# Linear attention with a channel-mix layer on one core: new instruction orders, wk columns read with a step, and two batches mixed on TensorE

## Chip, core and metric

The kernel runs on one core of a Trainium2 chip. The metric is the device time of one execution in microseconds. The engines are called by the names of the profile: PE is TensorE, DVE VectorE, ACT ScalarE, POOL GpSimd and SP SyncE. PEld is PE's weight load, which can run beside a matmul.

## What is computed

```python
# q, k, v: (8 batches, 8 heads, 576 rows, 64)
q_s = softmax(q, over the 64)
k_s = softmax(k, over the 576 rows)
kv  = einsum('bhsd,bhse->bhde', k_s, v)
x   = einsum('bhsd,bhde->bhse', q_s, kv)        # heads side by side: (8, 576, 512)
x_prev = x shifted by one row (zeros ahead of row 0)
xk = mu_k * x + (1 - mu_k) * x_prev
xr = mu_r * x + (1 - mu_r) * x_prev
k  = maximum(xk @ w_k, 0)                       # w_k: 512 x 1024
v  = (k * k) @ w_v                              # w_v: 1024 x 512
out = sigmoid(xr @ w_r) * v                     # w_r: 512 x 512
```

All inputs and the output are float32; the kernel multiplies in bf16.

## The kernel before

**Attention.** For each batch b and each of two groups g of four heads, `attention(b, g)` (L403) adds these steps. ACT takes the exponentials of q and k (L413) and casts v to bf16 (L419); DVE sums the exponentials of q by row, takes reciprocals and scales (L426, L429, L434); PE transposes the scaled q (L465, 36 small matmuls, each with its own weight load) into a PSUM bank `att`, and ACT copies it to `qt` (L470). PE multiplies k and v (L443, 36 small matmuls, the kv step) into another `att` bank (for batch 0 into two `mm` banks), and DVE takes the reciprocal of k's sums (L450, L454). These small matmuls use the PE array as four parts of 64x64.

**Mixing rows.** For the batches named in `ON_PE` (L36, only batch 0), DVE makes weights that hold kv, the reciprocal and mu or 1 - mu (`wps`, L515), and PE adds the present and the shifted rows in one bank: two pieces (h = 0, 1) for each of xk and xr (m = 0, 1), of 12 and 8 matmuls (L478 through L521). Each piece is evicted to `xk` or `xr` by the engine that `EVAC` names (L529). For the other batches PE makes x in two plain pieces of 4 matmuls (`w`, L556), ACT copies them to `xb` (L564), and DVE does the edge, the difference, four scalings by mu and two sums (L569 to L583).

**Channel mix.** Half of the batches (2304 rows) lie in a ring; `unit` (L613) takes them in pieces of 512, 512, 512, 512 and 256 rows. Per unit there are eight k steps (one for each 128 of the 1024 columns of w_k: four matmuls with a slice of `wk_bf` as weights and 512 or 256 rows of `xk` moving, L640), each followed by relu on ACT (L625) and a square on DVE (L629). Then, for each 128 rows, an r step (four matmuls, L671), tanh on ACT (L676), two v steps of four matmuls (L681), the gating on DVE (L687) and two stores from SP (L697). In the first two units of the first half, a k step is two halves: channel blocks 0 and 2, which need group 0, and 1 and 3, which need group 1. Four PSUM banks `mm` serve k, r and v; two pairs of banks `att` serve the attention.

**Loads.** The first batch's q, k and v come through ACT's and SP's queues in the order of `FIRST` (L30). All else is issued by POOL: wk in two parts (cast to bf16 on the way, each waiting for the load that `GATE` numbers), wr, the small mu load, wv in two parts, and the further batches, into 12 `raw` buffers.

**What sets the order.** No order is written out by hand. Each step is an `Op` with an engine, an occupation and a latency in microseconds, a key (due time) and the buffers that it takes. `Plan.order` (L120) walks a clock: for each engine it ranks what can start by start time (those within `LOOK` of the engine's free time count as equal) and key, and takes the earliest. `set_due` (L101) passes due times back from a step to what it needs, with `SPARE` more at each; `AHEAD` makes the mixes of batch 0, 1 and later due so much earlier; `PACE` spaces the due times of the matmuls. While PE was not busy for over 2.0 us of the last 3.4, its steps count twice. The order found is emitted as a fixed program.

Of the kernel before, what the change touches and what calls it, by code (L numbers as in the profile page):

```python
# [16 lines left out]
START = 0.7  # L17
HOP = 0.05
LATE = 1e6
SPARE = 0  # L20
LOOK = {"PE": 0.03, "ACT": 0.2, "DVE": 0.1, "POOL": 0.03, "SP": 0.03}
AHEAD = (1.0, 4, 8)
MAIN = 17.0
PACE = 1.148
DMA_RATE = 365.0
DMA_LEAD = 2.5
DMA_TAIL = 0.6

PARTS = {1: [slice(0, 2)], 2: [slice(0, 1), slice(1, 2)]}
FIRST = ((0, 0, ("ACT", "ACT")), (1, 0, ("SP", "SP")), (0, 1, ("ACT", "SP")),  # L30
         (0, 2, ("SP", "SP")), (1, 1, ("SP", "SP")), (1, 2, ("SP", "SP")))
ORDER = (0, 1, 2)
SOON = {(1, 0, 0): 2.2, (1, 0, 1): 2.4, (1, 1, 0): 2.7, (1, 0, 2): 3.5}
GATE = 6
FILL = 0
ON_PE = (0,)  # L36
CASTS = (("ACT", "ACT"), ("ACT", "ACT"))
EVAC = ((("ACT", "DVE"), ("ACT", "ACT")), (("ACT", "DVE"), ("ACT", "ACT")))


class Slot:
# [8 lines left out]
class Op:  # L50


    def __init__(self, engine, occ, lat, key, emit, deps, takes, gives, size):
        self.engine, self.occ, self.lat, self.key = engine, occ, lat, key
        self.emit, self.deps, self.takes, self.size = emit, list(deps), list(takes), size
        self.start = self.end = None
        self.early = 0.0
        for slot in gives:
            slot.last.append(self)


class Plan:
# [57 lines left out]
    def order(self):  # L120
        self.set_due()
        free = {}
        self.pe_busy = []
        dma_free = 0.0
        waiting = {}
        for op in self.ops:
            waiting.setdefault(op.engine, []).append(op)
        done = []
        left = len(self.ops)
        while left:  # L130
            chosen = None
            for engine, ops in waiting.items():
                now = free.get(engine, START)
                ready = None
                for op in ops:
                    if any(d.end is None for d in op.deps):
                        continue
                    t = max([now] + [d.end + HOP for d in op.deps])
                    ok = True
                    for slot in op.takes:  # L140
                        got = self.slot_time(slot)
                        if got is None:
                            ok = False
                            break
                        t = max(t, got[0] + HOP)
                    if not ok:
                        continue
                    rank = (max(t, now + LOOK[engine]), op.key)
                    if ready is None or rank < ready[0]:
                        ready = (rank, t, op)  # L150
                if ready is not None and (chosen is None or ready[1] < chosen[1]):
                    chosen = ready
            assert chosen is not None, "no operation can start"
            _, t, op = chosen
            for slot in op.takes:
                slot.index = self.slot_time(slot)[1]
                for part in self.pools[slot.pool][slot.index]:
                    self.user[part] = slot
            occ, lat = op.occ, op.lat
            if op.engine == "PE" and not self.warm(t):  # L160
                occ, lat = 2 * occ, occ + lat
            op.start, op.end = t, t + lat
            if op.size and op.size < 20:
                op.end = t + lat + (2.0 if op.engine == "SP" else 8.0)
            elif op.size:
                dma_free = max(dma_free, t + DMA_LEAD) + op.size / DMA_RATE
                op.end = dma_free + DMA_TAIL
            if op.engine == "PE":
                self.pe_busy.append((t, t + occ))
            free[op.engine] = t + occ  # L170
            waiting[op.engine].remove(op)
            done.append(op)
            left -= 1
        return sorted(done, key=lambda o: o.start)
# [3 lines left out]
def kernel(  # L178
# [81 lines left out]

    queues = {"SP": nc.sync, "ACT": nc.scalar, "POOL": nc.gpsimd}
    loaded = {}

# [22 lines left out]
    def emit_mu_load():  # L288
        for m, src in enumerate((moe_mu_k, moe_mu_r)):
            ap = bass.AP(tensor=src.tensor, offset=src.offset, ap=[[128, 4], [1, 128]])  # L290
            nc.gpsimd.dma_start(out=mu_sb[4 * m:4 * m + 4, :], in_=ap)

    def emit_warm():
        nc.scalar.activation(out=warm[:], in_=warm[:], func=ACT.Exp)
# [15 lines left out]
            nc.vector.memset(t[:, :, 0:1], 0.0)  # L310

    zero = plan.add("DVE", 0.1, 0.15, -10, emit_warm_zero)
    plan.add("ACT", 1.6, 1.7, 3.5, emit_warm, [zero])
    identity = plan.add("POOL", 0.6, 0.8, -9.1, emit_identity)
    consts = plan.add("DVE", 0.2, 0.3, -9, emit_consts, [identity])
    late_consts = plan.add("DVE", 0.14, 0.2, LATE, emit_late_consts)
# [16 lines left out]
                         rhs=mu_rows[:].rearrange("p m c -> p (m c)"), start=True, stop=True)  # L333

    def emit_mu_wide():
        nc.scalar.copy(out=mu_all[:, :, 0, :, :].rearrange("p m g c -> p m (g c)"),
                       in_=bank(rows_slot).rearrange("p (m c) -> p m c", m=2))

    def emit_mu_rest(m):
        nc.gpsimd.tensor_scalar(out=mu_all[:, m, 1, :, :], in0=mu_all[:, m, 0, :, :],  # L340
# [1 line left out]

    rows_load = plan.add("SP", 0.9, 0.9, -600, emit_mu_rows_load, size=10.0)
    rows_done = plan.add("PE", 0.86, 0.98, -501, emit_mu_rows, [rows_load, consts], [rows_slot])
    wide = plan.add("ACT", 0.48, 0.6, 0, emit_mu_wide, [rows_done], [], [rows_slot])
    mu_split = [plan.add("POOL", 0.5, 0.6, -2 + m, lambda m=m: emit_mu_rest(m), [wide])
                for m in range(2)]

# [24 lines left out]

    wk_done, wv_done = [], []
    for g in range(2):
        wk_done.append(plan.add("POOL", 0.75, 0.75, g, lambda g=g: emit_wk(g), gate,
                                size=1048.0))
    wr_done = plan.add("POOL", 0.75, 0.75, 2, emit_wr, gate, size=1048.0)
    mu_load = plan.add("POOL", 1.2, 1.2, 2.05, emit_mu_load, gate, size=8.0)
    mu_t = plan.add("PE", 0.2, 0.4, LATE, emit_mu, [mu_load, consts], [mu_slot])  # L380
    mu_done = plan.add("DVE", 0.08, 0.17, LATE, emit_mu_copy, [mu_t], gives=[mu_slot])

    def emit_wv(h):
        n = FT // 2
        ap = bass.AP(tensor=moe_w_v.tensor, offset=moe_w_v.offset + h * n * 128 * C,
                     ap=[[C, 128], [128 * C, n], [1, C]])
        nc.gpsimd.dma_start(out=wv_bf[:, h * n:(h + 1) * n, :], in_=ap)

    for h in range(2):
        wv_done.append(plan.add("POOL", 0.75, 0.75, 3 + h, lambda h=h: emit_wv(h), gate,  # L390
                                size=1048.0))
    for b in range(1, B):
        for g in range(2):
            for n, i in enumerate(ORDER):
# [8 lines left out]
    def attention(b, g):  # L403
# [63 lines left out]
                            in_=qss[qs.index][r, j, 64 * u:64 * u + 64], identity=ident[r, r])  # L467

        def copy_qt():
            nc.scalar.copy(out=qts[qt.index][:], in_=transposed()[:, :, 0:S])  # L470

        def by_heads(xp, parts):

# [13 lines left out]
        for n, u in enumerate(us):  # L487
# [10 lines left out]
            expk.append(plan.add("ACT", 0.09 + 0.96 * f, 0.2 + 0.96 * f, step + 1,  # L498
                                 lambda u=u: exp(eks, ek, sk, u), [lk[n]], [ek] if one else [],
                                 [sk]))  # L500
            if CASTS[min(b, 1)][n] == "ACT":
                castv.append(plan.add("ACT", 0.09 + 0.95 * f, 0.2 + 0.96 * f, step + 2,
                                      lambda u=u: cast_v(nc.scalar.copy, u), [lv[n], consts],
                                      [vv] if one else [], [sv]))
            else:
                castv.append(plan.add("DVE", 0.07 + 1.2 * f, 0.15 + 1.2 * f, step + 2,
                                      lambda u=u: cast_v(nc.vector.tensor_copy, u),
                                      [lv[n], consts], [vv] if one else [], [sv]))
        tr = plan.add("PE", 0.45, 0.62, pe_key, transpose_q, scaled + [identity], [qtp], [qs])
        qcopy = plan.add("ACT", 1.0, 1.12, step + 3, copy_qt, [tr], [qt], [qtp])  # L510
        kvm = plan.add("PE", 0.5, 0.6, pe_key, kv, expk + castv, [kvp], [ek, vv])
        zdone = plan.add("DVE", 0.08 * (2 if b == 0 else 1), 0.25 if b == 0 else 0.16, step + 2, recz, [kvm], [rz])

        def weights_of(wp, m, hf):
# [10 lines left out]
                     ((now, 0, 0, HS), (then, 0, 64, HS), (then, S - 64, 1, 64)))  # L525

        def copy_mixed(engine, xp, m, h):
            copy = nc.scalar.copy if engine == "ACT" else nc.vector.tensor_copy
            copy(out=xs[m][:, g::2, c0 + HS * h:c0 + HS * h + HS], in_=bank(xp)[:, :, 0:HS])  # L529

        if on_pe:
            for m in range(2):
# [6 lines left out]
                        for hf in range(2)]  # L539
                for h in range(2):  # L540
                    xp = Slot("att")
                    o = plan.add("PE", 0.29, 0.46, pe_key,
                                 lambda wp=wp, xp=xp, h=h: x_mixed(wp, xp, h), [qcopy] + made,
                                 [xp], [qt, wp])
                    e = EVAC[min(b, 1)][m][h]
# [36 lines left out]
        def mix(m):  # L582
# [1 line left out]
                                    in0=xms[xms_[m].index][:], in1=xbs[xb.index][:, :, 0:S],  # L584
                                    op=ALU.add)

        wdone = plan.add("DVE", 0.25, 0.35, step + 4, weights, [zdone, late_consts], [w],
                         [kvp, rz])
        evs = []
        for h in range(2):  # L590
            o = plan.add("PE", 0.16, 0.35, pe_key, lambda h=h: x(h),
                         [qcopy, wdone], [xps[h]], [qt, w])
            evs.append(plan.add("ACT", 0.52, 0.64, step + 5, lambda h=h: copy_x(h), [o],
                                [xb] if h == 0 else [], [xps[h]]))
# [18 lines left out]
    def unit(half, c0, n):  # L613
# [24 lines left out]
        def k_part(kf, fc, cts):  # L638
            for ct in cts:
                nc.tensor.matmul(bank(kf)[:, 0:n],  # L640
                                 lhsT=wk_bf[:, ct, fc * 128:(fc + 1) * 128],
                                 rhs=xs[0][:, ct, c0:c0 + n],
                                 start=(ct == 0), stop=(ct == CT - 1))

# [119 lines left out]
```

## Time and profile before

| | |
|---|---|
| median of 6 runs | 211.42 us (210.85 to 213.04) |
| the profiled execution: its time / its span | 211.94 / 210.2 us |
| PE busy | 187.3 us (89%) |
| PE weight loads busy | 90.1 us |
| DVE busy | 152.3 us (72%) |
| ACT busy | 150.6 us (72%) |
| POOL busy | 39.5 us |
| read from memory / written to it | 33.56 / 9.44 MB |
| share of PE in the chain that ended last | 76% |

The span runs from the first to the last recorded instruction; the execution's own time has 1.74 us more around it. In a timeline row stand the start, the duration, the engine, the line, the operation, what it writes and reads, the shape and how many rows were merged; in square brackets how long the engine stood idle before it and what, by the semaphores, ended that. A matmul's duration includes its way through the array, so the pace of matmuls is read from the distance of their starts. The granted clock is the share of full speed that PE was given. DMA moves nearly all the time until about 105 us, at about 400 GB/s between 35 and 75 us.

### The profile page before, as it was taken

The page shows a single profiled execution, that of the slowest core. Times are in us where ns is not written, and L with a number is a line of the kernel's source. Part 1 is how long each engine was busy: PE and PEld are TensorE (multiplying, and loading weights), DVE is VectorE, ACT ScalarE, POOL GpSimd, SP SyncE. Part 2 cuts the span into 40 slices and gives each one's busy share as a digit, 9 for nine tenths or more (in the row PEclk, how much of TensorE's full clock was granted, in tenths as well). Part 3 has the DMA queues.
Part 4 walks back from the last instruction along what each step waited for, and adds up shares of the span by engine and source line. Part 5 has one row for each costly group of instructions (what it writes and reads, how often), then busy time and mean ns, then how long its engine had stood idle before and what let it go on. Part 6 is the DMA issues. An engine that isn't in the chain of part 4 may idle for free.

```text
span 210.2 us, 5164 instructions
## 1 busy us (share of the span) xinstructions
PE 187.3 (89%) x2073; PEld 90.1 (43%) x2099; DVE 152.3 (72%) x338; ACT 150.6 (72%) x229; POOL 39.5 (19%) x63
## 2 busy tenths in 40 slices
PE   3188998948999989999997999999999999999991
PEld 0064444413444444454446443445444444444740
DVE  2683593999989999997749974976797369632531
ACT  4793998988999799999566987337993872452440
POOL 1471836534425112431000000000000000000000
PEclk9999999996999999999999999999999999999998
DMA  6999999999999997899442031242034103402514
GB/s 211 353 261 233 301 219 366 387 409 402 390 395 408 403 390 289 291 393 339 132 106 47 5 78 22 50 101 53 3 76 101 27 21 76 106 3 51 122 28 100
DMA packets 15856, 40.72 MB, mean 194 GB/s; under 512 B 2252, under 2 KB 3800, under 8 KB 15832
## 3 DMA queue, kind: packets, MB, share of 16 engines
q0 software_dynamic: 8336, 27.40, 38.9%
q1 hardware_dynamic: 7064, 12.10, 21.0%
q10 hardware_dynamic: 432, 0.88, 1.4%
q8 instruction: 16, 0.26, 0.5%
q14 instruction: 8, 0.07, 0.1%
HBM read 33.56 MB, written 9.44 MB: 205 GB/s over the span
## 4 chain that ended last, share of the span: by engine, by line
PE 76%; ACT 9%; DVE 9%; DMA 3%; issue 2%; ACTq 0%; DVEq 0%
PE mm_b L640 8%; PE mm_d L640 8%; PE mm_b L681 7%; PE mm_d L681 7%; PE mm_a L681 7%; PE mm_c L681 7%; PE mm_c L640 6%; PE mm_a L640 5%; PE mm_a L671 5%; PE mm_c L671 4%; PE mm_b L671 3%; DMA raw_b<-in_k_dram 3%; PE att_a L478 2%; PE att_b L478 2%; DVE qs_a L434 2%
## 5 line engine op out<-in xcount | busy, mean ns | idle before, releaser
L640 PEld LDWEIGHTS <-wk_bf 128*128 128x128 bf16 x320 | 30.8, 100 | 33.6 <-issue 5.7
L640 PE MATMUL mm_b<-xk,wk_bf 128*128 128x512 bf16 (+1 forms) x91 | 23.4, 365 | 1.8 <-DVE xk L583 1.7
L640 PE MATMUL mm_d<-xk,wk_bf 128*128 128x512 bf16 (+1 forms) x94 | 24.0, 368 | 0.2
L681 PEld LDWEIGHTS <-k_b 128*128 128x128 bf16 x144 | 13.5, 98 | 16.6 <-issue 1.1
L671 PEld LDWEIGHTS <-xr 128*128 128x128 bf16 x144 | 13.7, 98 | 15.8
L681 PEld LDWEIGHTS <-k_a 128*128 128x128 bf16 x144 | 13.3, 98 | 15.7 <-issue 0.9
L640 PE MATMUL mm_c<-xk,wk_bf 128*128 128x512 bf16 (+1 forms) x66 | 16.9, 365 | 0.6 <-issue 0.6
L640 PE MATMUL mm_a<-xk,wk_bf 128*128 128x512 bf16 (+1 forms) x60 | 14.9, 366 | 0.0
L671 PE MATMUL mm_a<-wr_bf,xr 128*128 128x512 bf16 x51 | 13.3, 379 | 0.1
L676 ACT ACTIVATE th_a<-mm_a 128x512 f32<-128x512 f32 x12 | 7.3, 607 | 6.5 <-PE mm_a L671 6.5
L671 PE MATMUL mm_c<-wr_bf,xr 128*128 128x512 bf16 x43 | 11.3, 380 | 0.1
L681 PE MATMUL mm_d<-wv_bf,k_a 128*128 128x512 bf16 x37 | 10.0, 379 | 0.6 <-issue 0.2
L681 PE MATMUL mm_b<-wv_bf,k_b 128*128 128x512 bf16 x37 | 10.0, 380 | 0.3 <-DVE rz_c L450 0.2
L681 PE MATMUL mm_a<-wv_bf,k_a 128*128 128x512 bf16 x39 | 10.1, 380 | 0.2 <-issue 0.2
L629 DVE TENSOR_TENSOR k_a<-rel_a 128x512 bf16<-128x512 bf16 (+1 forms) x13 | 5.1, 391 | 6.9 <-ACT rel_a L625 6.8
L681 PE MATMUL mm_d<-wv_bf,k_b 128*128 128x512 bf16 x39 | 9.9, 379 | 0.0
L676 ACT ACTIVATE th_b<-mm_c 128x512 f32<-128x512 f32 x8 | 4.9, 608 | 6.4 <-PE mm_c L671 6.3
L625 ACT ACTIVATE rel_b<-mm_d 128x512 bf16<-128x512 f32 (+1 forms) x12 | 7.1, 592 | 2.8 <-PE mm_d L640 2.2
L681 PE MATMUL mm_c<-wv_bf,k_b 128*128 128x512 bf16 x31 | 8.2, 380 | 0.1
L681 PE MATMUL mm_b<-wv_bf,k_a 128*128 128x512 bf16 x32 | 8.2, 379 | 0.0
L681 PE MATMUL mm_a<-wv_bf,k_b 128*128 128x512 bf16 x32 | 8.2, 379 | 0.0
L681 PE MATMUL mm_c<-wv_bf,k_a 128*128 128x512 bf16 x29 | 7.9, 380 | 0.3 <-DVE qs_b L434 0.2
(251 smaller groups left out, 420.1 us busy)
## 6 DMA issues: line engine op xcount, KB each, us to landing
out_dram<-ot_a SPq DMA_DIRECT2D x24, 128.0 KB, 2.4
out_dram<-ot_b SPq DMA_DIRECT2D x24, 128.0 KB, 2.4
out_dram<-ot_c SPq DMA_DIRECT2D x24, 128.0 KB, 2.4
raw_a<-in_q_dram POOLq DMA_DIRECT2D x3, 576.0 KB, 11.3
raw_c<-in_k_dram POOLq DMA_DIRECT2D x2, 576.0 KB, 10.4
raw_b<-in_v_dram POOLq DMA_DIRECT2D x2, 576.0 KB, 10.9
raw_d<-in_q_dram POOLq DMA_DIRECT2D x2, 576.0 KB, 10.8
raw_e<-in_k_dram POOLq DMA_DIRECT2D x2, 576.0 KB, 11.5
```

The source lines that it names most:

```text
L434: nc.vector.tensor_tensor(out=to[:, :, u, :], in0=eqs[eq.index][:, :, u, :], in1=by[:, :, :, None].to_broadcast((128, J, u.stop - u.start, ...
L478: nc.tensor.matmul(bank(xp)[64 * hf:64 * hf + 64, u, c:e], lhsT=w[r, hf, :], rhs=qts[qt.index][r, hf, src:src + e - c], start=(n == 0), st ...
L625: nc.scalar.activation(out=rels[rel.index][:, 0:n], in_=bank(kf)[:, 0:n], func=ACT.Relu, scale=HALF_ROOT)
L629: nc.vector.tensor_tensor(out=k2s[k2.index][:, fc, 0:n], in0=rels[rel.index][:, 0:n], in1=rels[rel.index][:, 0:n], op=ALU.mult)
L640: nc.tensor.matmul(bank(kf)[:, 0:n], lhsT=wk_bf[:, ct, fc * 128:(fc + 1) * 128], rhs=xs[0][:, ct, c0:c0 + n], start=(ct == 0), stop=(ct == ...
L671: nc.tensor.matmul(bank(rps), lhsT=xs[1][:, ct, c:c + 128], rhs=wr_bf[:, ct, :], start=(ct == 0), stop=(ct == CT - 1))
L676: nc.scalar.activation(out=ths[th.index][:], in_=bank(rps), func=ACT.Tanh, scale=0.5)
L681: nc.tensor.matmul(bank(vps), lhsT=k2s[k2.index][:, ft, 128 * m:128 * m + 128], rhs=wv_bf[:, ft, :], start=(ft == 0), stop=(ft == FT - 1))
```

## The change

Constants of the planner and durations of its steps are replaced, which remakes the order on every engine. Batch 1 joins batch 0 in `ON_PE`. Batch 0's evictions are split between DVE (h = 0) and ACT (h = 1). For the first group of batch 0, the copy of the transposed q goes to DVE and one half of v's cast to POOL; mu's wide copy goes to DVE. The small mu load goes from POOL to SP. A partition of `wv_bf` now holds eight neighbouring rows of w_v, four of which come in one run of 8 KB for each load, where it held rows 128 apart in runs of 2 KB; to match, a k step takes every eighth column of `wk_bf` as its weights. In the new program, PE has 64 more matmuls with their weight loads (4324 rows for 4196).

The stride and the wv load:

```diff
-        ap = bass.AP(tensor=moe_w_v.tensor, offset=moe_w_v.offset + h * n * 128 * C,
-                     ap=[[C, 128], [128 * C, n], [1, C]])
+        ap = bass.AP(tensor=moe_w_v.tensor, offset=moe_w_v.offset + h * n * C,
+                     ap=[[FT * C, 128], [C, n], [1, C]])
...
-                                 lhsT=wk_bf[:, ct, fc * 128:(fc + 1) * 128],
+                                 lhsT=wk_bf[:, ct, fc::FT],
```

Engines of steps, first loads and mix:

```diff
-FIRST = ((0, 0, ("ACT", "ACT")), (1, 0, ("SP", "SP")), (0, 1, ("ACT", "SP")),
+FIRST = ((0, 0, ("ACT", "ACT")), (0, 1, ("SP", "SP")), (1, 0, ("ACT", "SP")),
          (0, 2, ("SP", "SP")), (1, 1, ("SP", "SP")), (1, 2, ("SP", "SP")))
-SOON = {(1, 0, 0): 2.2, (1, 0, 1): 2.4, (1, 1, 0): 2.7, (1, 0, 2): 3.5}
-GATE = 6
+SOON = {(1, 0, 0): 1.2, (1, 1, 0): 1.5}
+GATE = 7
-ON_PE = (0,)
-CASTS = (("ACT", "ACT"), ("ACT", "ACT"))
-EVAC = ((("ACT", "DVE"), ("ACT", "ACT")), (("ACT", "DVE"), ("ACT", "ACT")))
+ON_PE = (0, 1)
+CASTS = (("POOL", "ACT"), ("ACT", "ACT"), ("ACT", "ACT"))
+QCOPY = ("DVE", "ACT", "ACT")
+WIDE = "DVE"
+MU_AT = 20
+EVAC = ((("DVE", "ACT"), ("DVE", "ACT")), (("DVE", "ACT"), ("DVE", "ACT")))
```

Planner constants and durations:

```diff
-SPARE = 0
-LOOK = {"PE": 0.03, "ACT": 0.2, "DVE": 0.1, "POOL": 0.03, "SP": 0.03}
-AHEAD = (1.0, 4, 8)
-PACE = 1.148
-DMA_RATE = 365.0
-DMA_LEAD = 2.5
-DMA_TAIL = 0.6
+SPARE = 0.3
+LOOK = {"PE": 0.2, "ACT": 0.2, "DVE": 0.03, "POOL": 0.03, "SP": 0.03}
+AHEAD = (3.0, 3, 2)
+PACE = 1.018
+DMA_RATE = 404.0
+DMA_LEAD = 1.75
+DMA_TAIL = 0.55
...
-                occ, lat = 2 * occ, occ + lat
+                occ, lat = op.cold * occ, lat + (op.cold - 1) * occ
...
-        tr = plan.add("PE", 0.45, 0.62, pe_key, transpose_q, scaled + [identity], [qtp], [qs])
+        tr = plan.add("PE", 0.306, 0.478, pe_key, transpose_q, scaled + [identity], [qtp], [qs])
+        tr.cold = 3.5
...
-        kvm = plan.add("PE", 0.5, 0.6, pe_key, kv, expk + castv, [kvp], [ek, vv])
+        kvm = plan.add("PE", 0.308, 0.478, pe_key, kv, expk + castv, [kvp], [ek, vv])
+        kvm.cold = 3.6
...
-                    o = plan.add("PE", 0.29, 0.46, pe_key,
+                    o = plan.add("PE", 0.27, 0.417, pe_key,
...
-            o = plan.add("PE", 0.16, 0.35, pe_key, lambda h=h: x(h),
+            o = plan.add("PE", 0.147, 0.3, pe_key, lambda h=h: x(h),
```

Loads on POOL, in their new order: the two parts of wk, q of batch 1 (both groups), wr, the two parts of wv, then k and v of batch 1. Before: wk, wr, the mu load, q and k of batch 1's first group, q of its second, then wv's parts with v between them, and the rest of batch 1.

## The prediction

> **What bounds the kernel now.** I read the table by stretches of time first, then the TensorE (PE) and VectorE (DVE) timelines where a stretch falls short, then the chain of waits (76% PE). The stretches, with the columns span, PE, PE weight loads, DVE, ScalarE (ACT), GpSimd (POOL), granted clock, DMA share, GB/s:
>
> ```profile
> 40.00:50.00 10.00, 6.25 (x132) 2.79 (x132) 9.86 (x19) 8.80 (x10) 4.30 (x6) 0.89 1.04 406
> 50.00:60.00 10.00, 9.80 (x123) 4.45 (x125) 9.49 (x22) 9.55 (x16) 4.33 (x6) 0.94 1.03 391
> 70.00:80.00 10.00, 9.13 (x185) 4.39 (x186) 9.95 (x21) 9.04 (x13) 1.44 (x2) 1.00 1.03 392
> 110.00:120.00 10.00, 8.50 (x187) 5.46 (x186) 9.98 (x28) 8.33 (x15) 0.00 (x0) 1.00 0.14 30
> ```
>
> PE is the bound nearly everywhere after 18 us. Only 40 to 50 us is bad: PE 6.25 of 10 while DVE is full, and the clock falls to 0.89 and 0.94. PE's and then DVE's timeline there:
>
> ```profile
> 42.84 0.61 PE L640 MATMUL mm_d<-xk,wk_bf 128*128 128x512 bf16 x2
> 45.08 0.48 PE L465 MATMUL att_b<-ident,qs_a 64*64 64x64 bf16 x36 [1.64 <-ACT vv_a L419]
> 45.39 0.50 PE L443 MATMUL att_a<-vv_a,ek_a 64*64 64x65 bf16 x36
> 47.61 0.50 PE L640 MATMUL mm_b<-xk,wk_bf 128*128 128x512 bf16 x1 [1.73 <-DVE xk L583]
> 48.34 1.06 PE L640 MATMUL mm_c<-xk,wk_bf 128*128 128x512 bf16 x2 [0.22 <-issue]
> 49.19 1.06 PE L640 MATMUL mm_d<-xk,wk_bf 128*128 128x512 bf16 x2
> ```
> ```profile
> 41.99 1.34 DVE L426 TENSOR_REDUCE rsum_a<-eq_b 128x18 f32<-128x1152 bf16 x1
> 43.67 1.36 DVE L434 TENSOR_TENSOR qs_a<-eq_b,rrec_a 128x1152 bf16<-128x1152 bf16 x1
> 44.94 0.19 DVE L569 COPY xb_b<-xb_b 128x126 bf16<-128x126 bf16 x1
> 46.81 0.75 DVE L583 TENSOR_TENSOR xk<-xm_c,xb_b 128x1152 bf16<-128x1152 bf16 x1
> ```
>
> Unit 2 (rows 512 to 1023) needs batch 1's xk. DVE puts batch 2's row sums and scaling before the mix of batch 1's second group, so PE stands twice and the next matmuls run at half speed: pairs start 0.85 us apart, later 0.43.
>
> **Prices on PE** (start to start, warm). Four 512-wide matmuls take 0.864 us, so 0.216 each; a 256-wide one takes 0.109. A block of 64x64 work costs extra[...]:
>
> ```profile
> 144.23 1.03 PE L640 MATMUL mm_b<-xk,wk_bf 128*128 128x512 bf16 x4
> 145.18 0.48 PE L465 MATMUL att_b<-ident,qs_a 64*64 64x64 bf16 x36
> 145.49 0.50 PE L465 MATMUL att_a<-ident,qs_b 64*64 64x64 bf16 x36
> 145.92 1.04 PE L640 MATMUL mm_d<-xk,wk_bf 128*128 128x512 bf16 x3
> ```
>
> 144.23 to 145.92 is 1.69; less 0.864 and two transposes of 0.31 leaves 0.2; shorter blocks give 0.16 to 0.21, so 0.19. A kv step is 0.31 too, a plain x piece (4 matmuls) 0.15, a mixed piece (8 or 12) 0.27 (20.85 to 21.12).
>
> **Opening, 0 to 27 us: about nothing (-0.2 us).** I walked the new order by hand with these durations and the old landings. ACT loses half of one v cast (0.57), one transposed-q copy (1.0) and the mu copy (0.5); DVE gains the last two (about 1.3 and 0.65 by its 0.65 per 576 columns from PSUM), so q of the second group is scaled at 13.7 us, not 12.6. But before, ACT freed itself for its copy only at 14.46; now it starts at 14.35. The first k matmul comes at 17.05 instead of 18.09, with five mixed pieces still to do instead of three, in more blocks: unit 1's k ends at 27.3, before 27.14. POOL's cast comes between the mu rows and the wk loads; it waits for the first v load (landed 9.3), and both wk loads queue behind it. POOL's rows of 256 columns took 0.40 and 0.90 us, so 576 columns cost 0.9 to 2.0; I take 1.4. Then wk is issued at about 10.7, not 9.55, behind raw loads that land until 13.0. That hides it; its first half is due at 17.05, and landed at 15.4. The two small mu loads leave POOL (1.1 us of issue) for SP, where they follow the last raw load: nothing waits there.
>
> **Loads.** Batch 1's k and v now stand behind wr and both wv parts on POOL. From 13.0 to 37 us the old run read 8.8 MB, about 366 KB/us; with 2.8 us per weight MB and 1.46 per raw tensor the new order lands wr at 24.4 (due 27.3), wv at 27.2 and 30.0 (due 29 and 31.6), the last v of batch 1 at 35.9. wv in runs of 8 KB instead of 2 KB: between no gain and 0.25 us per load (down to wr's 2.6); I take none, for no raw load with its longer runs shows what a casting one gains.
>
> **Batch 1's mix on PE.** Per group DVE loses edge 0.2, difference 0.67, four scalings 1.12, two sums 1.34 and w 0.2 (3.5 us), and gains four weights of 0.26 and two evictions of 0.65 (2.4); ACT's four copies stay four evictions, two of them DVE's. PE gains four pieces of 0.27 for two of 0.15. By the chain: last v at 35.9, cast to 37.05, q copy 38.1, two tanh and one exp to 40.1, eviction 41.4; unit 2 starts at 42.1, and its second channel half, which waits for DVE's eviction behind one row sum, at 43.45. That step was 47.61. PE waits 0.6 and 0.5 us there, too little to lower the clock.
>
> **From that step to PE's end.** Left in both: 137.0 us of dense matmuls (of 155.6).
> - Before: 22 transposes or kv (6.8), 24 pieces (3.6), 28 blocks (5.3): 47.61 + 152.7 = 200.3. PE ended at 205.43, so 5.1 is lost: half clock after 47.61 (1.6), waits at 74 to 77 (1.2) and 112 to 115 (1.7), small ones 0.6.
> - After: 24 (7.4), 24 plain and 4 mixed (4.7), 35 blocks (6.7; the order lists more single ones): 43.45 + 155.8 = 199.2. Waits: walking unit 2 I find 0.65 (kv waits for ACT's q copies; mm_b for a late gating). At the 256 unit a transpose needs the bank that ACT is emptying: 0.35; half a us for the rest. The waits of 74 and 112 go, for the kv steps no longer follow their transposes directly. Late mixes (DVE about 4.9 us after the last piece, PE 5.2 later) just fit. Total 200.7.
>
> **The strided wk columns.** Nothing in this trace reads weights with a step. The row with packed columns:
>
> ```profile
> L640 PEld LDWEIGHTS <-wk_bf 128*128 128x128 bf16 x320 | 30.8, 100 | 33.6 <-issue 5.7
> ```
> ```profile
> 109.22 2.52 PEld L640 LDWEIGHTS <-wk_bf 128*128 128x128 bf16 x24
> ```
>
> Loads are about 98 ns; under a 512-wide matmul (216) they hide with room, under the 64 256-wide ones (109) they nearly fill the time: 24 take 2.52 us. By the row a step costs 0. The Trainium skill speaks against it: "SBUF — State Buffer", section "Door 1: The DMA port swizzle", says that a 16-byte line of SBUF must be hit at least twice for full rate, and a step of 8 bf16 hits each line once. At half rate its price in "TensorE: Matmul & The Clock Gate", section "LDWEIGHTS (loading the stationary operand)", columns / 1.2 ns, gives an estimated 213 ns for 128 columns: 64 x 104 = 6.7 us. The same page ("Weight-path perf modes — Fast Weight Load (FWL) and DoubleRow") has 128 columns read as four parallel chunks of 32, strided too; 32 / 1.2 is 27 ns, and doubling adds 27 by estimate: 125 ns, 64 x 16 = 1.0 us. I take this, for 64-column loads here last as long (104 to 117 ns), so most of a load is not reading. Range 0 to 6.7; it cannot be a gain, since packed loads were hidden.
>
> **Sum.** 200.7 + 1.0 = 201.7 against 205.43: -3.7. The last gating and stores are alike (4.77 us). Span 210.2 - 3.7 = 206.5; with the 1.74 outside it the profiled execution (211.94) becomes 208.2. That one lies 0.52 above the median of 211.42, so 207.7.
>
> **Rivals.**
> - Slower, by the strided weight load alone. It decides at 109 + 4700/64 = 182 ns, where the 256-wide units eat the gain of 4.7. At 213 ns: 211.42 - 4.7 + 6.7 = 213.4; above 216 every ns costs all 320 loads. For: the line rule. Against: the long fixed part of a load. Chance 0.15.
> - No change: batch 1's loads come late. ACT's queue holds its k and v exps and casts, and behind them tanh and the evictions. Against it: the wv runs. For it: POOL stood 3.0 us waiting for wk's landing before issuing raw_i. 1.5 us later moves unit 2 by 1.5, and the clock falls again (1.6): 210.8. Chance 0.15.
> - Better: stepped loads are free, no new waits: 207.7 - 1.0 - 1.0 = 205.7. Chance 0.20.
>
> My forecast keeps 0.50. A measurement of this kernel can tell about 0.5% (1.06 us) from no change. Faster than 210.4: 0.48 + 0.20 + 0.03 = 0.71; within: 0.12; slower: 0.17. The range reaches below the better case, to 205.0, and up to 212.3, within the no-change case and part of the slower one.
>
> **What would show it.** Right: unit 2's second half starts near 43.5, the clock row of 40 to 60 us stays at 1.00, DVE falls below 9.8 in 40 to 50, no kv waits at 74 and 112, wk loads near 125 ns. Wrong: wk loads above 180 ns with 256-wide matmuls spread to match; ACT waiting for batch 1's k or v loads; the first k matmul after 18 us; kv or mixed pieces waiting for evictions in rows that I did not walk.

## The result, and the profile after

The kernel after takes 210.78 us (median, 209.44 to 212.26); the kernel before, run beside it, 211.81. The ratio is 0.9958 with a 95% interval from 0.9942 to 0.9974: 0.4% faster, where the prediction had 207.7 us, 1.8% faster. Ratios here compare fast executions alone, leaving out those over 1.5% above the fastest of their kernel, so they need not be the quotient of the medians, which are of all. The profiled execution has a time of 210.26 us and a span of 208.4.

The table by stretches of time of the kernel after (span, PE, weight loads, DVE, ACT, POOL, granted clock, DMA share, GB/s):

```profile
15.00:20.00 5.00, 2.25 (x34) 1.29 (x34) 2.28 (x6) 0.64 (x1) 1.37 (x3) 0.97 1.07 301
20.00:25.00 5.00, 5.00 (x46) 1.96 (x44) 1.92 (x3) 2.39 (x4) 2.40 (x5) 0.69 1.16 228
...
40.00:50.00 10.00, 9.08 (x141) 4.86 (x136) 8.96 (x16) 8.36 (x13) 3.61 (x5) 1.00 1.04 408
...
70.00:80.00 10.00, 9.79 (x147) 5.94 (x148) 9.98 (x19) 9.89 (x16) 3.02 (x5) 1.00 1.00 378
110.00:120.00 10.00, 9.58 (x122) 5.59 (x122) 9.27 (x24) 8.58 (x15) 0.00 (x0) 1.00 0.32 102
```

The hole that the prediction wanted gone is gone: in 40 to 50 us PE has 9.08 of 10 (6.25 before), DVE is no longer full and the clock is 1.00. The stretches at 70 and 110 have filled too. But 15 to 20 us, which had 4.47 of 5 before (the first row here), now has 2.25. After it PE's timeline in the kernel after, and then the timeline of its weight loads:

```profile
15.00:20.00 5.00, 4.47 (x70) 2.83 (x64) 2.12 (x8) 2.40 (x4) 1.08 (x2) 1.00 1.13 199
```
```profile
16.45 0.44 PE L645 MATMUL mm_c<-xk,wk_bf 128*128 128x512 bf16 x1
19.51 0.55 PE L483 MATMUL att_b<-qt_b,wp_c 64*64 64x288 bf16 x12 [2.62 <-DMA wk_bf<-in_moe_w_k_dram]
20.00 1.08 PE L645 MATMUL mm_d<-xk,wk_bf 128*128 128x512 bf16 x2
20.87 1.06 PE L645 MATMUL mm_a<-xk,wk_bf 128*128 128x512 bf16 x2
```
```profile
16.45 0.14 PEld L645 LDWEIGHTS <-wk_bf 128*128 128x128 bf16 x1 [0.39 <-DMA wk_bf<-in_moe_w_k_dram]
19.14 0.14 PEld L645 LDWEIGHTS <-wk_bf 128*128 128x128 bf16 x1 [2.55 <-DMA wk_bf<-in_moe_w_k_dram]
```

The same two weight loads in the kernel before run in a row, without a wait and before wk's second load is in (about 18.9):

```profile
17.69 0.13 PEld L640 LDWEIGHTS <-wk_bf 128*128 128x128 bf16 x2 [0.20 <-issue]
```

The first k half takes channel blocks 0 and 2, and both come in wk's first load. Its first weight load (block 0) runs at 16.45. Its second (block 2) stands for 2.55 us and starts when wk's *second* load lands, which brings only blocks 1 and 3. In the chain that ended last this is one long step, from that load's issue to its landing:

```profile
11.07 8.03 DMA wk_bf<-in_moe_w_k_dram
```

In the program five mixed pieces and all other k steps stand behind that weight load, and none of them starts before 19.14. Then the two-matmul steps start 0.87 us apart where full pace is 0.43; full pace comes back at 23.71, and unit 1's k ends at 29.71 (27.14 before). The waits for loads are put in when the program is built, from the slices that instructions read and write. The built program has this one in so many words; DMASW0 and DMASW1 count wk's two loads:

```
L645 Ldweights wk_bf [waits DMASW0_49]
L645 Matmult mm_c<-xk,wk_bf 128x512 [waits Activation_49]
L645 Ldweights wk_bf [waits DMASW1_49]
```

In the kernel before, the wait for DMASW1 comes first at blocks 1 and 3. So the explanation to be tested (theory A): the stepped slice of block 2 is taken to overlap the second load's target, `wk_bf[:, 1::2, :]`, which reaches from block 1 to block 3 with block 2 in between, although they share no element. The rivals: the wait is there, but what it delays is bound by batch 1's loads or ACT's queue anyway (B); or half of it comes back when the second load is truly due (C).

### The profile page after: what moved, and what is told of

Same layout as the page of the kernel before. It is cut to its first block, busy times and chain, and to the rows that moved or that the text cites. A ratio compares the mean times of both kernels' runs of the same rounds, so it can differ in the third digit from the quotient of the medians.

```text
span 208.4 us, 5298 instructions
## 1 busy us (share of the span) xinstructions
PE 188.0 (90%) x2135; PEld 102.2 (49%) x2163; DVE 152.8 (73%) x336; ACT 148.4 (71%) x224; POOL 38.6 (19%) x62
## 4 chain that ended last, share of the span: by engine, by line
PE 79%; DMA 8%; DVE 5%; ACT 2%; issue 2%; POOL 0%; SPq 0%; DVEq 0%; ACTq 0%
PE mm_b L686 9%; PE mm_c L686 8%; PE mm_c L645 8%; PE mm_a L645 7%; PE mm_d L686 7%; PE mm_b L645 7%; PE mm_d L645 6%; PE mm_a L686 6%; PE mm_a L676 5%; PE mm_d L676 4%; DMA wk_bf<-in_moe_w_k_dram 4%; PE mm_b L676 3%; DMA raw_d<-in_v_dram 3%; PE mm_c L676 3%; PE att_a L483 2%
## 5 line engine op out<-in xcount | busy, mean ns | idle before, releaser
L645 PEld LDWEIGHTS <-wk_bf 128*128 128x128 bf16 x320 | 42.7, 145 | 22.8 <-DMA wk_bf<-in_moe_w_k_dram 2.9
L645 PE MATMUL mm_c<-xk,wk_bf 128*128 128x512 bf16 (+1 forms) x90 | 22.0, 359 | 0.2
L645 PE MATMUL mm_a<-xk,wk_bf 128*128 128x512 bf16 (+1 forms) x77 | 20.5, 374 | 0.3 <-issue 0.2
L686 PEld LDWEIGHTS <-k_b 128*128 128x128 bf16 x144 | 13.0, 98 | 15.4 <-issue 1.1
L645 PE MATMUL mm_d<-xk,wk_bf 128*128 128x512 bf16 (+1 forms) x73 | 18.6, 364 | 0.3 <-issue 0.2
L645 PE MATMUL mm_b<-xk,wk_bf 128*128 128x512 bf16 (+1 forms) x72 | 17.5, 361 | 0.0
L676 PE MATMUL mm_d<-wr_bf,xr 128*128 128x512 bf16 x44 | 11.3, 379 | 0.1
L634 DVE TENSOR_TENSOR k_b<-rel_a 128x512 bf16<-128x512 bf16 (+1 forms) x14 | 5.4, 388 | 3.7 <-ACT rel_a L630 3.4
L681 ACT ACTIVATE th_b<-mm_d 128x512 f32<-128x512 f32 x8 | 4.8, 596 | 3.9 <-PE mm_d L676 3.1
L681 ACT ACTIVATE th_b<-mm_b 128x512 f32<-128x512 f32 x7 | 4.2, 600 | 4.4 <-PE mm_b L676 4.3
L676 PE MATMUL mm_b<-wr_bf,xr 128*128 128x512 bf16 x28 | 7.2, 379 | 0.0
```

Of the source, the lines that this page charges most:

```text
L634: nc.vector.tensor_tensor(out=k2s[k2.index][:, fc, 0:n], in0=rels[rel.index][:, 0:n], in1=rels[rel.index][:, 0:n], op=ALU.mult)
L645: nc.tensor.matmul(bank(kf)[:, 0:n], lhsT=wk_bf[:, ct, fc::FT], rhs=xs[0][:, ct, c0:c0 + n], start=(ct == 0), stop=(ct == CT - 1))
L676: nc.tensor.matmul(bank(rps), lhsT=xs[1][:, ct, c:c + 128], rhs=wr_bf[:, ct, :], start=(ct == 0), stop=(ct == CT - 1))
L681: nc.scalar.activation(out=ths[th.index][:], in_=bank(rps), func=ACT.Tanh, scale=0.5)
L686: nc.tensor.matmul(bank(vps), lhsT=k2s[k2.index][:, ft, 128 * m:128 * m + 128], rhs=wv_bf[:, ft, :], start=(ft == 0), stop=(ft == FT - 1))
```

## The experiments

All ratios are to the kernel before on the same chip, with 95% intervals. "Second half" is the first k step of unit 2 on blocks 1 and 3, the step that the prediction followed.

**Two tiles for wk.** One tile per load, so that no slice can touch the other load; all else as after.

```diff
-    wk_bf = const.tile([128, CT, F], BF16, name="wk_bf")
+    wk_bfs = [const.tile([128, CT // 2, F], BF16, name=f"wk_bf{x}") for x in "pq"]
...
-        ld = nc.gpsimd.dma_start(out=wk_bf[:, g::2, :], in_=ap)
+        ld = nc.gpsimd.dma_start(out=wk_bfs[g][:], in_=ap)
...
-                                 lhsT=wk_bf[:, ct, fc::FT],
+                                 lhsT=wk_bfs[ct % 2][:, ct // 2, fc::FT],
```

> The kernel after, with wk in two SBUF tiles, one per load; orders, step and wv's runs stay. Theory A (the first k unit waits for wk's second load only because the stepped slice of the first load's columns is taken to overlap the second load's part of the same tile): the second weight load no longer waits, PE works on from 16.5 us, the granted clock of 15 to 25 us comes back from 0.97 and 0.69 to about 1.00, unit 1's k ends near 27.3 instead of 29.7, unit 2's second half starts near 43.4 instead of 45.7, and the time falls by 2 to 2.5 us: ratio to the kernel before 0.984 to 0.988, about 208.2. Rival B (the wait was there, but what it delays is bound by batch 1's loads and ScalarE's queue anyway): unit 2's second half stays within 0.7 us of 45.7 and the ratio stays at 0.993 to 0.996. Rival C (TensorE waits for wk's second load a little later, at the third k half, so half of the wait comes back): ratio near 0.990.

Measured: 208.17 us, ratio 0.9803 (0.9756 to 0.985). Its opening, the first two weight loads of k and PE's timeline:

```profile
15.91 0.34 PEld L645 LDWEIGHTS <-wk_bfp 128*128 128x128 bf16 x2 [0.20 <-issue]
```
```profile
16.10 0.38 PE L645 MATMUL mm_c<-xk,wk_bfp 128*128 128x512 bf16 x1
16.62 0.44 PE L483 MATMUL att_b<-qt_b,wp_c 64*64 64x288 bf16 x12
17.00 0.65 PE L645 MATMUL mm_d<-xk,wk_bfp 128*128 128x512 bf16 x2
17.49 0.59 PE L645 MATMUL mm_a<-xk,wk_bfp 128*128 128x512 bf16 x2
```

No pause, and full pace from the start (0.49 apart). Unit 1's k ends at 25.91, the second half starts at 41.91. A holds; B falls, since the second half moved by as much as unit 1's k; C falls, since PE has no wait for wk's second load at all: blocks 1 and 3 come up at 19.34, when that load is in.

**No step at all.** wk's columns and wv's rows as before; orders and mix as after; wk in one tile again.

```diff
-        ap = bass.AP(tensor=moe_w_v.tensor, offset=moe_w_v.offset + h * n * C,
-                     ap=[[FT * C, 128], [C, n], [1, C]])
+        ap = bass.AP(tensor=moe_w_v.tensor, offset=moe_w_v.offset + h * n * 128 * C,
+                     ap=[[C, 128], [128 * C, n], [1, C]])
...
-                                 lhsT=wk_bf[:, ct, fc::FT],
+                                 lhsT=wk_bf[:, ct, fc * 128:(fc + 1) * 128],
```

> The kernel after with contiguous wk columns again and wv's old rows (runs of 2 KB): no step anywhere, the new orders and the mix of two batches kept. Theory A (the false wait is the step's only cost, its 145 ns weight loads are hidden): the same as the kernel with wk in two tiles within 0.3%, so a ratio of about 0.985 to 0.988; wk weight loads near 100 ns; wv's loads up to 0.25 us longer each, hidden. Rival (the longer weight loads do cost, 64 of them about 16 to 36 ns each beyond the matmul): 1 to 2.3 us faster than the kernel with two wk tiles. Rival (wv's longer runs are worth something): slower than that kernel by the time that batch 1's last load lands later, 0.3 to 1 us.

Measured: 207.96 us, ratio 0.9798 (0.9748 to 0.9847), unit 1's k ends at 25.84, second half at 42.25. The same as with two tiles: neither the longer stepped weight loads nor wv's longer runs move the time by anything that can be seen here. It also shows that a contiguous slice of the one interleaved tile has no false wait; the first two weight loads run together once wk's first load is in:

```profile
16.15 0.13 PEld L645 LDWEIGHTS <-wk_bf 128*128 128x128 bf16 x2 [0.20 <-DMA wk_bf<-in_moe_w_k_dram]
```

**The step in the old orders.** The kernel before with the two edits of the step alone (the diff above the other way round).

> The kernel before with the stepped wk columns and wv's runs of rows alone; its orders stay. Theory A: in the old order k starts at 18.09 us and wk's second load lands at about 18.9, so the false wait costs 0.5 to 1 us there, in a stretch where PE has other work: ratio 1.000 to 1.006, with the wait for wk's second load at the second weight load of k, and matmuls of 256 columns still 109 ns apart. Rival (stepped weight loads slow the 256-wide units): ratio 1.008 or more, with 256-wide matmuls spread to 125 to 145 ns. Rival (wv's runs carry the gain): ratio below 0.997 and earlier landings of the last raw load.

Measured: 212.65 us, ratio 0.9968 (0.9929 to 1.0007). The same wait stands at the second weight load of k. It is shorter than in the kernel after, since wk's second load is in at 17.89 and not at 19.14; the first weight load comes at nearly the same time (16.59 and 16.45). The weight loads:

```profile
16.59 0.14 PEld L640 LDWEIGHTS <-wk_bf 128*128 128x128 bf16 x1 [0.20 <-issue]
17.89 1.29 PEld L640 LDWEIGHTS <-wk_bf 128*128 128x128 bf16 x7 [1.15 <-DMA wk_bf<-in_moe_w_k_dram]
```

That the wait is there in the old orders too says that the step alone makes it. What it costs there can't be told from zero: the interval reaches past 1, and in this execution unit 1's k even ends at 25.93, before the 27.14 of the kernel before. Its middle, 0.9968, would also suit the rival that wv's longer runs gain a little; the interval doesn't decide that, and the two kernels above, with and without the longer runs, show no such gain. The 256-wide steps stay 0.43 us apart per four matmuls (107.52 to 107.95), so the weight loads don't slow them.

**The mix alone.** The kernel before with `ON_PE = (0, 1)`, nothing else.

> The kernel before with batch 1's mix on PE alone; everything else stays, with the old measured times in the planner and the old priorities. If the mix by itself carries the gain: unit 2's second half starts at 44 to 45.5 us instead of 47.61 and the ratio is 0.985 to 0.992. If it needs the new orders (ScalarE's four evictions queued behind batch 1's exps and casts, kv directly after its transposes): ratio 0.997 to 1.01, with TensorE waiting for evictions or q copies between 36 and 50 us.

Measured: 209.15 us, ratio 0.9854 (0.9803 to 0.9905); second half at 45.18 (47.61 before), PE 8.96 of 10 in 40 to 50 us. Most of the gain needs one constant, and not the new orders.

**The kernel after again**, on the chip of the next three.

> The kernel after, unchanged, beside the next three on one chip. Its ratio to the kernel before was 0.9958 with 0.9942 to 0.9974; both theories expect 0.992 to 0.998 here again, about 210.8 us, and the profile again with a pause of about 2.6 us at the second weight load of the first k unit.

Measured: 210.81 us, ratio 0.9934 (0.9904 to 0.9964); pause 2.2 us, unit 1's k ends at 30.17, second half at 46.17. In this execution the granted clock of 15 to 25 us reads 1.00, and yet the two-matmul steps start 0.87 us apart:

```profile
20.00:25.00 5.00, 5.00 (x43) 2.01 (x42) 1.47 (x3) 1.67 (x3) 2.70 (x5) 1.00 1.12 234
```
```profile
20.99 1.08 PE L645 MATMUL mm_d<-xk,wk_bf 128*128 128x512 bf16 x2
21.86 1.04 PE L645 MATMUL mm_a<-xk,wk_bf 128*128 128x512 bf16 x2
```

So the clock row is no full record of PE's pace; the distance of starts is.

**One tile, each load's blocks side by side.** The tile keeps the blocks in the order 0, 2, 1, 3, the step stays.

```diff
-        ld = nc.gpsimd.dma_start(out=wk_bf[:, g::2, :], in_=ap)
+        ld = nc.gpsimd.dma_start(out=wk_bf[:, 2 * g:2 * g + 2, :], in_=ap)
...
-                                 lhsT=wk_bf[:, ct, fc::FT],
+                                 lhsT=wk_bf[:, 2 * (ct % 2) + ct // 2, fc::FT],
```

> The kernel after with wk in one tile still, but with each load's two channel blocks beside each other (blocks in the order 0, 2, 1, 3) and not alternating with the other load's; the step of 8 columns stays. If the false wait comes from the stepped slice's span reaching over blocks of the other load that lie between (slice taken as everything from its first to its last element): no pause at the second weight load, and the same time as with two tiles, ratio 0.978 to 0.987. If any stepped slice is taken to depend on all of its tile: the pause stays, ratio 0.993 to 0.998.

Measured: 209.30 us, ratio 0.983 (0.9782 to 0.9878). PE's timeline:

```profile
17.24 1.07 PE L645 MATMUL mm_c<-xk,wk_bf 128*128 128x512 bf16 x2 [0.95 <-DMA wk_bf<-in_moe_w_k_dram]
18.24 0.69 PE L483 MATMUL att_b<-qt_b,wp_c 64*64 64x288 bf16 x12
```

Both matmuls of the first half run together (x2); the 0.95 us ahead of them is a true wait, for wk's first load. So it is not the shared tile, and not the step by itself: it takes a stepped slice *and* another load's blocks interleaved with it. Whether they must lie on both sides of the slice no run separates, and how the build comes to the overlap stays open.

**Batch 1's mix back on DVE.** Two wk tiles, `ON_PE = (0,)`, the rest as after.

> The kernel with wk in two tiles, with only batch 0's mix on PE (batch 1's back on DVE), everything else as in the kernel after. Theory A (the mix of batch 1 is what frees DVE between 40 and 50 us, 3.5 us of DVE work less, unit 2's second half at 41.9 instead of 47.6): unit 2's second half starts 2 to 4 us later than with the mix on PE, DVE above 9.7 in 40 to 50, and the ratio is 0.992 to 1.000. Rival (the new orders alone carry the gain and the mix only moves work): the ratio stays below 0.987.

Measured: 210.92 us, ratio 0.9883 (0.9819 to 0.9947). The stretch, and PE's timeline in it:

```profile
40.00:50.00 10.00, 6.63 (x66) 3.01 (x63) 9.91 (x20) 8.24 (x11) 3.86 (x6) 0.85 1.04 409
```
```profile
43.00 0.65 PE L645 MATMUL mm_a<-xk,wk_bfp 128*128 128x512 bf16 x2 [1.39 <-DVE xk L588]
...
46.32 0.48 PE L448 MATMUL att_a<-vv_a,ek_a 64*64 64x65 bf16 x36 [1.80 <-ACT vv_a L424]
46.73 0.94 PE L645 MATMUL mm_a<-xk,wk_bfq 128*128 128x512 bf16 x2
```

The old hole is back: DVE full, PE at 6.63, clock 0.85, second half at 46.73. Place and sign as theory A had them. The ratio is lower than the 0.992 to 1.000 that it expected, and its interval stays below 1, so the new orders carry something of their own.

**The old orders with mix and step.** The mix alone, plus two wk tiles, the step and wv's rows.

> The old orders with batch 1's mix on PE, and with the stepped wk columns, wk in two tiles and wv's runs of rows: it lacks only the new orders, opening and measured times of the kernel with two wk tiles (0.9803). If those are worth little, as the 0.9854 of the mix alone suggests: ratio 0.983 to 0.988. If step and wv's runs carry a gain that the mix alone did not have: ratio 0.978 to 0.982. If the opening and the orders are worth 2 us: 0.988 or more.

Measured: 210.53 us, ratio 0.991 (0.9873 to 0.9947), second half at 45.10. The mix alone had 0.9854 (0.9803 to 0.9905). The intervals meet, the second half starts at nearly the same time, and no wait in the trace accounts for 0.5%; whether step and wv's runs cost something in these orders stays open. They bring nothing.

**Two tiles once more**, beside the next three.

> The kernel with wk in two tiles once more, beside the next three on one chip. The first time its ratio was 0.9803 (0.9756 to 0.985), and the kernel with one tile and each load's blocks side by side gave 0.983. If both measure the same thing: 0.978 to 0.986 here. What may differ between executions: in the first profile PE worked at full pace from 16.6 us, in the other only from 22.3, after a pause of 1.0 us for wk's first load.

Measured: 207.56 us, ratio 0.9798 (0.9751 to 0.9845). The profiled execution is the slowest of its six (209.13 us), where the first time it was the fastest of six (207.30): half pace until 22.70, unit 1's k ends at 28.70 and not 25.91, the second half starts at 44.70, the span is 207.4 and not 205.5. The same program, then, reaches full pace at 16.6 in one execution and at 22.7 in another. PE here (two-matmul steps 0.87 us apart until the last of these rows):

```profile
18.58 1.07 PE L645 MATMUL mm_d<-xk,wk_bfp 128*128 128x512 bf16 x2
19.45 1.06 PE L645 MATMUL mm_a<-xk,wk_bfp 128*128 128x512 bf16 x2
...
22.70 0.65 PE L645 MATMUL mm_c<-xk,wk_bfq 128*128 128x512 bf16 x2
```

**The pause filled.** The kernel after, with work for PE inside the false wait, at the first k half alone.

```diff
...
+                if fill is not None and ct == 2:
+                    for _ in range(24):
+                        nc.tensor.matmul(bank(fill)[:, 0:128], lhsT=ident[:], rhs=ident[:],
+                                         start=True, stop=True)
...
```

> The kernel after with its false wait, but with 24 matmuls of 128 columns on the identity (their result is overwritten) between the first k matmul and the second weight load, which fill about 2.6 us at half pace or 1.3 us at full pace. It tells what the wait costs beside its own length. If half of the loss is slow matmuls after the pause (pairs 0.86 apart until 22.8 to 23.7 us): PE works at full pace from about 19 us, unit 1's k ends 1.0 to 2.3 us earlier than 29.7 to 30.2, ratio 0.985 to 0.990. If the pause alone is the loss: ratio 0.993 to 0.998. If the filling outlasts the wait: above that.

Measured: 208.64 us, ratio 0.9853 (0.9804 to 0.9902), between the kernel after (0.9934 and 0.9958, not run beside it) and the one without the wait (0.9798). That points to a good part of the loss being slow matmuls after the pause. The trace can't confirm it: in its profiled execution, the slowest of the six, wk's first load came late as well (first k matmul at 18.48), and the filling, at half pace, took 2.77 us and outlasted the wait. The share of pace in the loss stays open.

**The opening filled.** Two wk tiles, and 16 matmuls on the identity after the first group's kv.

```diff
+            if b == 0 and g == 0:
+                for _ in range(16):
+                    nc.tensor.matmul(kv_of(kvp, 0)[:, 128:256], lhsT=ident[:], rhs=ident[:],
+                                     start=True, stop=True, skip_group_check=True)
```

> The kernel with wk in two tiles, with 16 matmuls of 128 columns on the identity added after the first group's kv, where PE has stood 1.0 to 1.2 us for the scaled q of the second group; nothing reads their result. If the slow matmuls of the opening are PE not having worked long enough without a hole: full pace by 15 to 16 us in every execution, 0.5 to 1.5 us faster than the kernel with two tiles on the same chip, ratio 0.973 to 0.980. If that is settled otherwise or already so in most executions: the same within 0.3%. If the filling delays the second group's transposes: up to 0.7 us slower.

Measured: 208.63 us, ratio 0.9815 (0.9755 to 0.9874): no gain to be seen. The idea of full pace by 15 to 16 us in every execution falls: in the profiled one, the second slowest of six, PE stood 1.8 us for wk's first load and ran at half pace until 23.75, though this kernel has no false wait.

**A step of 4.** Two wk tiles; a k step takes every fourth column of one half of F.

```diff
-                                 lhsT=wk_bfs[ct % 2][:, ct // 2, fc::FT],
+                                 lhsT=wk_bfs[ct % 2][:, ct // 2, 512 * (fc // 4) + fc % 4:512 * (fc // 4) + 512:4],
...
-        ap = bass.AP(tensor=moe_w_v.tensor, offset=moe_w_v.offset + h * n * C,
-                     ap=[[FT * C, 128], [C, n], [1, C]])
+        ap = bass.AP(tensor=moe_w_v.tensor, offset=moe_w_v.offset + h * 512 * C,
+                     ap=[[4 * C, 128], [C, n], [1, C]])
```

> The kernel with wk in two tiles, with a step of 4 columns in place of 8 (each block of 128 columns lies in one half of F; wv's loads keep runs of 4 rows). It asks what sets the duration of a stepped weight load: 98 ns packed, 145 ns at a step of 8. If each 16 bytes of SBUF read cost a share (a step of 4 uses two of eight numbers in 16 bytes, a step of 8 one): between, near 98 to 120 ns. If any step costs the same: 145 ns. For the time every theory that has stepped loads hidden expects the same as the kernel with two tiles within 0.3%.

Measured: 207.75 us, ratio 0.9796 (0.9748 to 0.9844). The groups of weight loads (busy us, mean ns) of this kernel, and then that of the kernel after:

```profile
L645 PEld LDWEIGHTS <-wk_bfp 128*128 128x128 bf16 x160 | 17.8, 114 | 15.0 <-issue 2.4
L645 PEld LDWEIGHTS <-wk_bfq 128*128 128x128 bf16 x160 | 17.8, 115 | 12.7 <-issue 0.4
```
```profile
L645 PEld LDWEIGHTS <-wk_bf 128*128 128x128 bf16 x320 | 42.7, 145 | 22.8 <-DMA wk_bf<-in_moe_w_k_dram 2.9
```

Packed 98 to 100 ns, step 4 114 to 115, step 8 145, and the same time for all three (0.9798, 0.9796, 0.9803): the duration follows the step, the kernel's time doesn't. That 114 lies between suits the theory that each 16 bytes read cost a share, and not the one that any step costs the same.

## Why the prediction was wrong

**The step that failed is the opening**, "about nothing (-0.2 us)", and in it the sentence on wk: "its first half is due at 17.05". The orders were walked with the data that each step needs; the wait that the step's own access pattern adds was left at nothing. In times it costs 1.0 to 1.6%, or 2.2 to 3.4 us: the kernel after has 0.9958 and 0.9934, the four kernels with the new orders, the mix and no false wait (two tiles, no step, blocks side by side, step of 4) 0.980 to 0.983. No rival named it, although the built program of the kernel after has it among its waits.

In the traces unit 1's k was to end at 27.3. With the false wait it ended at 29.71 and 30.17, mean 29.9; in the five profiled executions without it at 25.91 and 28.70 (two tiles), 25.84, 28.70 and 27.81, mean 27.4. The difference of 2.5 us agrees with the times, but the five spread by 2.9: against the executions that also run at half pace until 22.70 the wait costs 1.0 to 1.5 us, against those at full pace from the start about 4. So the predicted 27.3 is met on the mean and by no single execution; as the prediction says nothing of the pace that decides between them, part of that is luck.

The opening's loss carries through to the end. The second half started 1.9 us earlier than before (47.61 to 45.72), and the span is 1.8 us shorter; the prediction had 4.2 and 3.7. It asked for 0.9824 (207.7 / 211.42), and that total is right for the kernel without the false wait, though two of its smaller terms were off and cancel (below).

The other steps:

- **Terms of the opening.** POOL's cast was taken at 1.4 us and took 0.66; DVE's copy of the transposed q, taken at 1.3, took 0.70. wk was issued at 10.18, not 10.7, but its first load was in only at 16.45, not at the old 15.4; the first k matmul came at 16.45 against 17.05.
- **Loads, and the rival of late loads.** From the end of unit 1's k to the second half the prediction had 27.3 to 43.45, 16.15 us. Measured: 16.0 in the kernel after (29.71 to 45.72), 16.0 with two tiles (25.91 to 41.91; 28.70 to 44.70), 16.0 with blocks side by side, 16.4 without the step. A stretch that keeps its length while its start moves by 4 us is set by the core's own engines, not by what lands: in the chain of the kernel after PE's steps run to 41.7, and DVE's from there to the end of the eviction at 45.66. That rival gave nearly the measured time (210.8) for a reason that did not occur.
- **Batch 1's mix on PE.** Right: DVE's eviction for the second half follows one row sum, as predicted:

```profile
43.65 1.34 DVE L431 TENSOR_REDUCE rsum_a<-eq_b 128x18 f32<-128x1152 bf16 x1
44.91 0.75 DVE L534 CAST xk<-att_a 128x576 bf16<-128x576 f32 x1
```

- **From the second half to PE's end.** Predicted 157.25 us and 1.0 for the step, 158.25; measured 158.1 (45.72 to 203.78, where the record of the last matmuls ends). As the step measured nothing, the rest was put 0.8 us too low: two errors that cancel. The waits at 74 and 112 us went, as the stretches at 70 and 110 show: between 28 and 125 us PE stood 2.1 us at kv steps for copies of the transposed q in the kernel before, and 0.2 us in the kernel after.
- **The stepped weight load.** Its duration was put too low (125 ns, measured 145), its price too high (1.0 us, measured nothing). The 256-wide k steps of the kernel after, and their weight loads:

```profile
107.34 0.60 PE L645 MATMUL mm_d<-xk,wk_bf 128*128 128x256 bf16 x4
107.78 0.60 PE L645 MATMUL mm_b<-xk,wk_bf 128*128 128x256 bf16 x4
```
```profile
106.84 1.74 PEld L645 LDWEIGHTS <-wk_bf 128*128 128x128 bf16 x16
```

Four matmuls in 0.44 us are 110 ns each, where the kernel before has 109. Sixteen weight loads of 140 ns or more would fill 2.24 us end to end and take 1.74, so each starts before the last one ends. A load longer than its matmul need not stretch the pace to its own length, and the break-even of the slower rival, worked out as if it did, does not hold at 145 ns; longer loads no run has. The line rule of the Trainium skill ("SBUF — State Buffer", section "Door 1: The DMA port swizzle"), which spoke against the change, has its direction confirmed by 98, 114 and 145 ns. Its limits are not: a step of 4 hits each line twice, which the rule calls enough, and costs 16 ns all the same; and the next sentence there has a step of up to 8 bf16 free, where 145 ns are measured. That a longer load costs PE's pace no run shows.

**What the parts are worth.** The old orders with the mix have 0.9854, the new ones without it 0.9883, both together 0.980. Each does more than half of the work alone, so the two overlap. Only the mix fills the hole at 40 (PE 8.96 of 10 with the mix alone, 6.63 with the new orders alone, 6.25 before). Both clear the kv waits at 74 and 112: PE stands 0.4 us for copies of the transposed q with the mix alone and none with the new orders alone, 2.1 before. That this is all of the overlap is argued, not shown. The step brought nothing in any pair of kernels, and in the kernel after it took back 1.0 to 1.6 of the 2.0% that the rest gains. Two tiles for wk, or leaving the step out, beats both kernels: 207.6 to 208.2 us.

## What to carry to other kernels

When a change alters how a tile is sliced, look at the waits of the built program and not only at the data that each step needs: a stepped slice between two parts of another load's target can wait for that load, though they share no element. Lay out what arrives together side by side, or in a tile of its own. A weight load that grows by half (98 to 145 ns here) can be free; measure the distance of matmul starts, not the load.

## What was not expected of the hardware

- PE's pace in the opening differs between executions of one program: full pace from 16.6 us or from 22.7 (two tiles, twice), while the granted clock of 20 to 25 us can read 0.69 or 1.00 over matmuls at the same half pace (the kernel after, twice). The Trainium skill ("TensorE: Matmul & The Clock Gate", section "Part 1: The HAM clock gate (the "warmup" mystery)") says that PE's speed is set by a free-running window of about 3.4 us of activity, so that one kernel changes over at different moments. That executions differ agrees; the section puts the variation at 0.5 us either way for matmuls without a break, and in this opening, where PE also pauses, it is 6.1 us. The window itself no run here shows. One profiled execution of such an opening is no basis for differences below 2 to 3 us.
- The duration of a weight load of 128 columns follows the step: 98 ns packed, 114 at 4, 145 at 8, at an unchanged pace of 110 ns per 256-wide matmul.
- DVE copies 1152 bf16 from PSUM in 0.70 us where ACT takes 1.12, and POOL casts 576 columns from float32 to bf16 in 0.66 to 0.94.
